# Uneven dV stores around one DMA engine, x in two pieces, and a reordered tail in a decode gradient kernel

## The chip, the cores and the metric

The kernel runs on one core of a Trainium2 chip. The metric is the device time of one execution in microseconds. A core has five compute engines (PE, the tensor engine; DVE, the vector engine; ACT, the scalar engine; POOL, the general engine; SP, which here only issues transfers) and sixteen DMA engines that carry all transfers. SP, ACT and POOL issue transfers, each into a queue of its own.

## The reference

The forward function mixes two branches over one token x of 640 numbers: a decode attention with 32 heads over a cache of 4096 keys and values of 128 numbers, and a dense layer with a Mish activation. The kernel computes the output and the gradients (a vector-Jacobian product with grad_out) of nine inputs.

```python
def forward(x, k_cache, v_cache, wq, wo, B_x, w1, b1, w2, gate_w):   # bfloat16
    g = sigmoid((x * gate_w).sum(-1, keepdims=True))
    q = (x @ wq).reshape(32 heads, 128)
    p = softmax(q . k_cache * 128 ** -0.5)           # 32 x 4096
    a = (p . v_cache).reshape(1, 4096) @ wo
    h = B_x @ w1 + b1
    b = (h * tanh(softplus(h))) @ w2
    return g * a + (1 - g) * b
# outputs: the result, then d/dx, dK, dV (each 32 x 4096 x 128), dwq, dwo, dw1, db1, dw2, dgate_w
```

K and V are read once (32 MB each) and dK and dV written once (32 MB each). With the weights and their gradients the page counts 82.03 MB read and 82.03 MB written.

## The kernel before

Heads are taken in 16 pairs; `NP` is 16 and `J` is 64. K or V of a pair is one tile of 128 partitions by 8192 bfloat16 numbers, 16 KB a row and 2 MB in all. There are seven such buffers (`bufs`, named `kv0` to `kv6`). A gradient is written over the tile that it belongs to: dV over V, dK over K, in four quarters by `outer` (line 465, on DVE), and then stored to memory from the same buffer. Free buffers wait in `free_q`. `pump` starts the next loads of a fixed list, all on SP, whenever a buffer is given back; the instruction on SP then waits until the store out of that buffer has landed. `store_kv` (line 736) issues one store and gives its buffer back; the stores go by POOL while loads are left and by SP afterwards.

The order of all other work is written out by hand. The function `slot(i, s)` has the sixteen steps of pair i: transposes of V and of the next K on PE (line 374) with copies out of PSUM on ACT (line 377), products for the scores and for dP (line 384), the softmax, column sums for o and dq (line 433), and the quarters of dV and dK. A table `side`, filled by `plan` and `at`, hangs the weights' work on these steps: the dense branch in pairs 0 to 6, and wo, wq and their gradients spread over the rest, in four groups of eight heads.

At the start POOL issues five small loads one after the other (line 185): x, gate_w, grad_out and b1 in two parts. At the end the last pair is written out without `slot`. The helper `last_dv(t)` makes quarter t of dV and, after the second and the fourth quarter, stores half of it through SP (line 875); `last_dk(t)` does the same for dK (line 881). Between them stand the rows of dwo (`dwo_row`, on ACT, stored through ACT by `st_dwo`), the last sums for dx (`dx_sum`, line 486), the last part of dwq (`dwq_row` on ACT, stored by `st_dwq` through POOL) and `o_rows` and `a_cols`, which turn the last heads' o into wo's products. Then a short chain of small steps makes the three small outputs out, dx and dgate_w: `fin` is collected on DVE (lines 918 to 935) with a sum over partitions on PE in between (`dg_ps`, line 928), transposed on PE (`fr_ps`, line 939), copied by DVE into `frow` (line 941) and stored by three transfers on POOL (line 944).

Of the kernel before, what the change touches and what calls it, by code (L numbers as in the profile page):

```python
# [17 lines left out]
def kernel(  # L18
# [34 lines left out]
    P = 128  # L53
    _, H, Sk, Dh = A_k_cache.shape
# [5 lines left out]
    J = 64  # L60
# [22 lines left out]
    dwo_v = out_5.rearrange("(g p k) n -> g p k n", p=P, k=8)  # L83
# [3 lines left out]
    def vec_cols(v):  # L87
        return v.rearrange("(p c) -> p c", c=RC)

    x_v = A_x.rearrange("a b (p c) -> (a b p) c", c=RC)  # L90
    dy_v = grad_out.rearrange("a b (p c) -> (a b p) c", c=RC)
# [10 lines left out]
    def C(shape, dt, name):  # L102
        return const.tile(shape, dt, name=name, tag=name)
# [3 lines left out]
    bufs = [big.tile([P, bufw.get(i, KVW)], BF16, name=f"kv{i}", tag=f"kv{i}") for i in range(NBUF)]  # L107
    wqa = big.tile([P, RC, H * Dh], BF16, name="wq", tag="wq")
    wob = [big.tile([P, 8, D], BF16, name=f"wo{i}", tag=f"wo{i}") for i in range(2)]
    tch = [chp.tile([P, 4, P, 2], BF16, name=f"tch{i}", tag=f"tch{i}") for i in range(NT)]  # L110

    xc = C([P, RC], BF16, "xc")
    dyc = C([P, RC], BF16, "dyc")
    gwc = C([P, RC], BF16, "gwc")
# [7 lines left out]
    kbuf, vbuf, mbuf = {}, {}, {}  # L122
# [48 lines left out]
    def pump():  # L171
        while loads and (free_q or not loads[0][0]):
            loads.popleft()[1]()
# [5 lines left out]
        base=0, pattern=[[-1, P]], channel_multiplier=1,  # L179
    )  # L180
    pump()
    for t, src in ((xc[:], x_v), (gwc[:], vec_cols(gate_w)), (dyc[:], dy_v),
                   (b1c[:, 0:FK], B_b1[0:FM].rearrange("(p k) -> p k", k=FK)),
                   (b1c[0:FR, FK:FN], B_b1[FM:F].rearrange("(p o) -> p o", o=1))):
        nc.gpsimd.dma_start(t, src)
# [34 lines left out]
    def misc(shape, dt, name):  # L220
        return one_ps.tile(shape, dt, name=name, tag="misc")

    def chain(shape, dt, name):
        return one_ps.tile(shape, dt, name=name, tag="chain")
# [99 lines left out]
    def o_rows(g):  # L324
        ps = misc([P, 16, 8], F32, "o8_ps")
        nc.tensor.matmul(ps[:].rearrange("p a b -> p (a b)"), lhsT=od16[:].rearrange("p a b -> p (a b)"), rhs=idb[:],
                         start=True, stop=True)
        o8m = two.tile([P, 16, 8], F32, name="o8m", tag="o8m", bufs=1)
        nc.vector.tensor_tensor(o8m[:], ps[:], m16[:].unsqueeze(2).to_broadcast([P, 16, 8]), ALU.mult)
        nc.vector.reduce_sum(o8f[:], o8m[:].rearrange("p a b -> p b a"), axis=AX.X)  # L330
        nc.vector.tensor_copy(o8[:], o8f[:])

    def a_cols(g, c0=0, c1=RC):
        if c0 == 0:
            mst["a"] = misc([P, RC + W], F32, "a_ps")
        ps = mst["a"][:, 0:RC]
        wv = wob[g % 2][:].rearrange("p k (n c) -> p k c n", c=RC)
        for c in range(c0, c1):
            for k in range(8):
                nc.tensor.matmul(mst["a"][:, c:c + W], lhsT=wv[:, k, c, :], rhs=o8[:, k:k + 1].to_broadcast([P, W]),  # L340
                                 start=(k == 0), stop=(k == 7))
        if c1 == RC:
            if g == 0:
                nc.vector.tensor_copy(a_acc[:], ps)
            else:
                nc.vector.tensor_tensor(a_acc[:], a_acc[:], ps, ALU.add)

    def scaled(eng, dst, src, col):
        if eng is nc.vector:
            nc.vector.tensor_scalar(dst, src, col, None, ALU.mult)  # L350
        else:
            nc.scalar.mul(dst, src, col)  # L352
# [1 line left out]
    def dwo_row(g, k, eng=nc.scalar):  # L354
        scaled(eng, wob[g % 2][:, k, :], da_bc[:], o8f[:, k:k + 1])

    def st_dwo(g, eng, k0=0, k1=8):
        eng.dma_start(dwo_v[g][:, k0:k1], wob[g % 2][:, k0:k1])


    def kview(b):
# [18 lines left out]
    def products(ps, src, c, col):  # L380
        for t in range(4):
            B = 4 * c + t
            for e in range(2):
                nc.tensor.matmul(ps[:, 4 * B:4 * B + W].rearrange("p (a b) -> p a b", b=4),  # L384
                                 lhsT=src[:, t, :, e],
                                 rhs=col[:, e, :, :].rearrange("p a b -> p (a b)").unsqueeze(1).to_broadcast([P, W // 4, 4]),
                                 start=(e == 0), stop=(e == 1))
# [74 lines left out]
    def outer(b, col, row, q):  # L462
        n = J // 4
        j0 = q * n
        nc.vector.tensor_tensor(  # L465
            kview(b)[:, j0:j0 + n, :].rearrange("p j (a b) -> p j a b", b=2),
            col[:, j0:j0 + n, :].unsqueeze(2).to_broadcast([P, n, Dh // 2, 2]),
            row.rearrange("p (a b) -> p a b", b=2).unsqueeze(1).to_broadcast([P, n, Dh // 2, 2]),
            ALU.mult)
# [5 lines left out]
    def dq_row(i):  # L475
        dqb = two.tile([P, 2], BF16, name="dqb", tag="dqb")
        nc.vector.tensor_copy(dqb[:], st[i]["dq"][:, 0:2])  # L477
        ps = chain([P, 2, P], BF16, "dqr_ps")
        for hh in range(2):
            nc.tensor.transpose(ps[:, hh, :], dqb[:, hh:hh + 1].to_broadcast([P, P]), idb[:])  # L480
        c = 256 * (i % 4)
        nc.scalar.copy(dqrow[(i // 4) % 2][:, c:c + 256].rearrange("p (a b) -> p a b", a=2), ps[:])
# [6 lines left out]
    def dwq_row(g, c0, c1, rc, eng=nc.scalar):  # L489
        scaled(eng, wqa[:, rc, g * GC + c0:g * GC + c1], dqrow[g % 2][:, c0:c1], xf[:, rc:rc + 1])  # L490

    def st_dwq(c0, c1, eng):
        eng.dma_start(dwq_v[:, :, c0:c1], wqa[:, :, c0:c1])
# [178 lines left out]
    for k in range(8):  # L672
        at(4, (6, 7, 9, 10, 11, 11, 13, 14)[k], dwo_row, 0, k, nc.vector if k in (4, 5, 6, 7) else nc.scalar)
    plan(4, {5: rows(mlp_dxb, 0), 7: rows(mlp_dxb, 1), 14: rows(mlp_dxb, 2)})
    plan(5, {0: [(st_dwo, 0, nc.gpsimd)], 1: [(ld_wo, 2)], 5: rows(mlp_dxb, 3), 7: rows(mlp_dxb, 4), 14: dx(0, 0, 0, GC, 0)})
    plan(4, {10: [(ld_wq, HC, 2 * HC, nc.scalar)]})
    plan(6, {0: [(st_dw1,)]})

    for g in range(NG - 1):
        i = 4 * g + 4  # L680
# [16 lines left out]
    for g in (2, 3):  # L697
        i = 4 * g
# [8 lines left out]
    g, i = NG - 1, NP - 2  # L707
# [14 lines left out]
    def run_products(i, s):  # L722
# [5 lines left out]
        else:  # L728
# [2 lines left out]
                S_ps[n] = one_ps.tile([P, 2 * J + W], F32, name="S", tag="S")  # L731
            products(S_ps[n], src, s - 8, qR[(n // 4) % 2][:, n % 4])

    def store_kv(dct, i, dst, eng):
        b = dct[i]
        eng.dma_start(dst, bufs[b][:, 0:J * Dh])  # L736
        free_q.append(b)
        pump()

# [3 lines left out]
    def slot(i, s):  # L743
# [16 lines left out]
        if chain_on:  # L760
            if s == 0:
                dq_row(i - 1)
            if s in (0, 1, 3):
                dk_quarter(i - 1, (0, 1, 3).index(s) + 1)
            if s == 3:
                store_kv(kbuf, i - 1, dKv[i - 1], nc.gpsimd if loads else nc.sync)
            if s == 2:
                soft_max(i)
            if s == 4:
                soft_maxt(i)  # L770
            if s == 7:
                soft_z(i)
# [9 lines left out]
        if s in (9, 10, 12, 13):  # L782
            outer(vbuf[i], st[i]["p"], Dr[(i // 4) % 2][:, i % 4, :], (9, 10, 12, 13).index(s))
            if s == 13:
                store_kv(vbuf, i, dVv[i], nc.gpsimd if loads else nc.sync)
# [81 lines left out]
    i, g = NP - 1, NG - 1  # L867
# [3 lines left out]
    def last_dv(t):  # L871
        outer(vbuf[i], st[i]["p"], Dr[g % 2][:, q, :], t)
        if t % 2:
            h = slice((t - 1) * KVW // 4, (t + 1) * KVW // 4)
            nc.sync.dma_start(dVv[i][:, h], bufs[vbuf[i]][:, h])

    def last_dk(t):
        outer(fb, st[i]["ds"], Qr[g % 2][:, q, :], t)
        if t % 2:
            h = slice((t - 1) * KVW // 4, (t + 1) * KVW // 4)  # L880
            nc.sync.dma_start(dKv[i][:, h], bufs[fb][:, h])
# [12 lines left out]
    last_dv(0)  # L894
    for rc in range(RC):
        dwq_row(g, CA, CB, rc)
    o_rows(g)
    dq_row(i)
    last_dv(1)
    a_cols(g)  # L900
    for k in range(8):
        dwo_row(g, k)
        if k % 4 == 3:
            st_dwo(g, nc.scalar, k - 3, k + 1)
    last_dv(2)
    last_dv(3)
    last_dk(0)
    last_dk(1)
    for rc in range(RC):
        dx_sum(g, NG + g, CB, GC, rc)  # L910
        dwq_row(g, CB, GC, rc)
    st_dwq(g * GC + CA, (g + 1) * GC, nc.gpsimd)
    last_dk(2)
    last_dk(3)

    fin = C([P, 3, RC], BF16, "fin")
    ga = C([P, RC], F32, "ga")
# [8 lines left out]
                                   accum_out=dgp[:])  # L926
    dg_ps = chain([P, 1], F32, "dg_ps")
    nc.tensor.matmul(dg_ps[:], lhsT=ones_f[:], rhs=dgp[:], start=True, stop=True)
    dz = C([P, 1], F32, "dz")
    nc.vector.tensor_scalar(dz[:], dg_ps[:], g_all[:], omg[:], ALU.mult, ALU.mult)  # L930
    nc.vector.tensor_scalar(fin[:, 2, :], xf[:], dz[:], None, ALU.mult)
# [5 lines left out]
    fr_ps = misc([3, RC, P], BF16, "fr_ps")  # L937
    for c in range(RC):
        nc.tensor.transpose(fr_ps[:, c, :], fin[:, :, c], idb[:])
    frow = C([3, P, RC], BF16, "frow")  # L940
    nc.vector.tensor_copy(frow[:].rearrange("r p c -> r c p"), fr_ps[:])
    for r, v in enumerate((out_0.rearrange("a b n -> (a b) n"), out_1.rearrange("a b n -> (a b) n"),
# [31 lines left out]
```

## Time and profile before

| what | value |
|---|---|
| median of three runs | 406.26 us (405.51 to 407.17) |
| the profiled execution | 405.83 us |
| its span, first to last instruction | 404.0 us |
| busy: PE, weight loads, DVE, ACT, POOL | 297.2, 272.9, 285.6, 246.8, 25.2 us |
| DMA: moved, mean rate | 164.88 MB, 408 GB/s |
| DMA queue q1 (SP) | 8832 packets, 94.08 MB |
| DMA queue q0 (POOL) | 5472 packets, 63.42 MB |
| DMA queue q10 (ACT) | 1602 packets, 6.56 MB |
| DMA queue q8 (instructions) | 44 packets, 0.72 MB |

The busy times are shares of one span and overlap. A transfer between a tile of 128 rows and memory is spread over the sixteen DMA engines; each engine moves its share, 8 rows for such a tile, and then reports on its own, so that a transfer has sixteen landing times and counts as landed with the last of them. In the profile's stretches, a busy share of 1.00 stands for all sixteen DMA engines and 0.06 for one.

### The profile page before, as it was taken

Reading aid. Unit: us, or ns where it says so; the run is one execution under the profiler, and the core shown is the slowest. Engines: PE = TensorE matmul, PEld = TensorE weight load, DVE = VectorE, ACT = ScalarE, POOL = GpSimd, SP = SyncE. Lnnn points to the kernel's source line nnn. Section 1 sums busy time; section 2 is a strip of 40 time slices with the busy share of each in tenths; the row PEclk is TensorE's granted clock in tenths of the full one; section 3 lists DMA queues with packets and bytes.
Section 4 is the critical chain, followed back from the end, with each engine's and each line's share of the span. In section 5 each row is a group of like instructions: output and inputs, shape, how many; then the busy total and the mean of one; then the engine's idle time right before and its main releaser. Section 6 shows DMA issues by size and latency. Waiting matters only on the chain.

```text
span 404.0 us, 13041 instructions
## 1 busy us (share of the span) xinstructions
PE 297.2 (74%) x5654; PEld 272.9 (68%) x5657; DVE 285.6 (71%) x618; ACT 246.8 (61%) x507; POOL 25.2 (6%) x50
## 2 busy tenths in 40 slices
PE   4878996998885888673989869732989897987110
PEld 3558986877775777673889769732789786886100
DVE  2767695699975969583797839642695988597930
ACT  3555462586668678761766567731567996876800
POOL 3000100002000101000001000000000100000020
PEclk9999997998999899986999989985899998999555
DMA  8999999999999999999999999999999999999991
GB/s 275 426 399 434 420 423 417 430 418 420 423 422 427 391 421 429 427 431 430 428 423 428 426 427 426 425 426 432 431 406 400 414 428 419 422 430 422 420 386 44
DMA packets 15963, 164.88 MB, mean 408 GB/s; under 512 B 1713, under 2 KB 1905, under 8 KB 6178
## 3 DMA queue, kind: packets, MB, share of 16 engines
q1 hardware_dynamic: 8832, 94.08, 55.7%
q0 software_dynamic: 5472, 63.42, 37.3%
q10 hardware_dynamic: 1602, 6.56, 4.1%
q8 instruction: 44, 0.72, 0.7%
q14 instruction: 13, 0.11, 0.1%
HBM read 82.03 MB, written 82.03 MB: 406 GB/s over the span
## 4 chain that ended last, share of the span: by engine, by line
DMA 34%; issue 23%; PE 20%; DVE 12%; ACT 5%; POOL 2%; SPq 1%; POOLq 0%; ACTq 0%; DVEq 0%
DMA wq<-in_A_wq_dram 10%; DMA out_dram<-kv 8%; PE tr L374 8%; DVE kv L465 7%; DMA wq<-in_B_w_dram 6%; DMA wo<-in_A_wo_dram 5%; DMA kv<-in_A_k_cache_dram 5%; ACT tch L377 2%; PE dP L384 2%; PE o L433 2%; PE S L384 2%; PE dq L433 1%; PE q_ps L277 1%; PE a_ps L340 1%; DVE wq L486 1%
## 5 line engine op out<-in xcount | busy, mean ns | idle before, releaser
L374 PE MATMUL tr<-idf,kv 128*128 128x128 f32 x1024 | 172.1, 294 | 36.0 <-DMA kv<-in_A_v_cache_dram 20.0
L377 ACT COPY tch<-tr 128x512 f32<-128x512 f32 x256 | 144.2, 587 | 83.8 <-PE tr L374 78.6
L374 PEld LDWEIGHTS tr<-idf,kv 128*128 128x128 f32 x1024 | 118.6, 150 | 41.7 <-issue 36.9
L384 PEld LDWEIGHTS <-tch 128*128 128x128 bf16 x2048 | 89.5, 99 | 27.9 <-ACT tch L377 21.8
L465 DVE TENSOR_TENSOR kv<-p_dup,Dr 128x2048 bf16<-128x2048 bf16 x64 | 76.7, 1220 | 4.4 <-ACT p_dup L424 4.1
L465 DVE TENSOR_TENSOR kv<-ds_dup,Qr 128x2048 bf16<-128x2048 bf16 x64 | 76.8, 1220 | 0.4
L433 PEld LDWEIGHTS <-kv 128*128 128x128 bf16 x2048 | 59.1, 97 | 2.7 <-issue 1.6
L384 PE MATMUL dP<-dR,tch 128*128 128x48 bf16 x1024 | 47.3, 185 | 9.3 <-ACT tch L377 9.0
L384 PE MATMUL S<-qR,tch 128*128 128x48 bf16 x1024 | 48.1, 187 | 6.9 <-ACT tch L377 5.7
L290 DVE SCALAR_TENSOR_TENSOR junk<-wo,da_bc 128x640 bf16<-128x640 bf16 x32 | 26.3, 822 | 13.5 <-DMA wo<-in_A_wo_dram 12.7
L433 PE MATMUL o<-e_m,kv 128*128 128x48 bf16 x1024 | 32.4, 186 | 0.2 <-issue 0.2
L433 PE MATMUL dq<-ds_m,kv 128*128 128x48 bf16 x1024 | 30.6, 183 | 2.1 <-DVE ds_m L455 1.9
L736 POOL DMA_DIRECT2D out_dram<-kv x25 | 13.4, 537 | 296.0 <-DVE kv L465 278.6
L352 ACT ACTIVATE wq<-dqrow,xf 128x1024 bf16<-128x1024 bf16 (+2 forms) x30 | 25.1, 860 | 1.2 <-DVE wq L486 0.8
L486 DVE SCALAR_TENSOR_TENSOR wq<-wq,dqrow 128x1024 bf16<-128x1024 bf16 (+2 forms) x30 | 25.1, 863 | 0.2
L439 DVE TENSOR_TENSOR o<-o,rz 128x2 f32<-128x2 f32 x16 | 2.5, 158 | 26.5 <-PE o L433 26.5
L398 DVE TENSOR_REDUCE m<-S 64x1 f32<-64x64 f32 x32 | 7.0, 219 | 15.8 <-PE S L384 15.6
L424 ACT ACTIVATE p_dup<-e_m,rz 64x128 bf16<-64x128 bf16 x32 | 12.7, 397 | 7.8 <-DVE rz L418 7.4
L352 ACT ACTIVATE wo<-da_bc,o8f 128x640 bf16<-128x640 bf16 x20 | 15.9, 824 | 1.5 <-PE a_ps L340 0.9
L406 DVE TENSOR_REDUCE negM<-mt 64x1 f32<-64x64 f32 x32 | 7.1, 222 | 11.5 <-PE mt L403 10.8
L480 PE MATMUL dqr_ps<-idb,dqb 128*128 128x128 bf16 x32 | 4.9, 241 | 13.7 <-DVE dqb L477 13.7
L459 ACT COPY ds_dup<-ds_m 64x128 bf16<-64x128 bf16 x32 | 9.5, 297 | 8.1 <-DVE ds_m L455 7.6
(163 smaller groups left out, 253.2 us busy)
## 6 DMA issues: line engine op xcount, KB each, us to landing
out_dram<-kv POOLq DMA_DIRECT2D x25, 2048.0 KB, 19.8
kv<-in_A_v_cache_dram SPq DMA_DIRECT2D x16, 2048.0 KB, 19.8
kv<-in_A_k_cache_dram SPq DMA_DIRECT2D x15, 2048.0 KB, 20.6
out_dram<-kv SPq DMA_DIRECT2D x5, 2048.0 KB, 26.2
wo<-in_A_wo_dram SPq DMA_DIRECT2D x4, 1280.0 KB, 20.9
out_dram<-kv SPq DMA_DIRECT2D x4, 1024.0 KB, 20.5
out_dram<-wo POOLq DMA_DIRECT2D x3, 1280.0 KB, 26.8
wq<-in_A_wq_dram SPq DMA_DIRECT2D x2, 1280.0 KB, 9.5
```

The costliest lines, as they stand in the source:

```text
L290: nc.vector.scalar_tensor_tensor(junk[:], in0=wob[g % 2][:, k, :], scalar=1.0, in1=da_bc[:], op0=ALU.mult, op1=ALU.mult, accum_out=do8[g % ...
L352: nc.scalar.mul(dst, src, col)
L374: nc.tensor.transpose(tp[:, t, :], src[:, 4 * c + t, :], idf[:])
L377: nc.scalar.copy(dst[:].rearrange("p a b e -> p (a b e)").bitcast(F32), tp[:].rearrange("p a b -> p (a b)"))
L384: nc.tensor.matmul(ps[:, 4 * B:4 * B + W].rearrange("p (a b) -> p a b", b=4), lhsT=src[:, t, :, e], rhs=col[:, e, :, :].rearrange("p a b - ...
L406: nc.vector.tensor_reduce(negM[HS[hh]], mt[HS[hh], 64 * hh:64 * hh + 64], axis=AX.X, op=ALU.max, negate=True)
L424: nc.scalar.activation(p[HS[hh]], e_m[i % 2][HS[hh], :, hh].unsqueeze(2).to_broadcast([64, J, 2]), ACT.Copy, scale=st[i]["rz"][HS[hh], hh: ...
L433: nc.tensor.matmul(st[i][key][:].rearrange("p (a b) -> p a b", b=2), lhsT=src[:, j, :], rhs=rhs[:, j, :].unsqueeze(1).to_broadcast([P, W / ...
L459: nc.scalar.copy(ds[HS[hh]], ds_m[i % 2][HS[hh], :, hh].unsqueeze(2).to_broadcast([64, J, 2]))
L465: nc.vector.tensor_tensor(kview(b)[:, j0:j0 + n, :].rearrange("p j (a b) -> p j a b", b=2), col[:, j0:j0 + n, :].unsqueeze(2).to_broadcast ...
L486: nc.vector.scalar_tensor_tensor(w, in0=w, scalar=1.0, in1=dqrow[g % 2][:, c0:c1], op0=ALU.mult, op1=ALU.mult, accum_out=dq_acc[:, rc, par ...
L736: eng.dma_start(dst, bufs[b][:, 0:J * Dh])
```

## The change

Three things change. First, `store_kv` stores dV of pairs 5 and 10 in three transfers instead of one: rows 0 to 1, 2 to 121 and 122 to 127 for pair 5, and rows 0 to 10, 11 to 115 and 116 to 127 for pair 10. They are issued one after the other on POOL, and by the change's own words the sizes are such that DMA engine 4 is left out of the large piece. Second, the load of x at the start becomes two loads, of rows 0 to 59 and 60 to 127. Third, in the tail `last_dv(1)` stands ahead of `o_rows` and `dq_row`, `last_dv(2)` ahead of `a_cols`, `last_dk(1)` behind the last sums for dx, and `last_dk(2)` and `last_dk(3)` stand inside the chain that makes the small outputs, behind the matmul of `dg_ps` and behind the transposes of `fr_ps`. The parameter `rows` that `st_dwo` gains has its default everywhere, which is one transfer as before.

```diff
-    for t, src in ((xc[:], x_v), (gwc[:], vec_cols(gate_w)), (dyc[:], dy_v),
+    for t, src in ((xc[0:60], x_v[0:60]), (xc[60:P], x_v[60:P]), (gwc[:], vec_cols(gate_w)), (dyc[:], dy_v),
...
-    def st_dwo(g, eng, k0=0, k1=8):
-        eng.dma_start(dwo_v[g][:, k0:k1], wob[g % 2][:, k0:k1])
+    def st_dwo(g, eng, k0=0, k1=8, rows=(P,)):
+        p0 = 0
+        for n in rows:
+            eng.dma_start(dwo_v[g][p0:p0 + n, k0:k1], wob[g % 2][p0:p0 + n, k0:k1])
+            p0 += n
...
+    uneven = {5: (2, 120, 6), 10: (11, 105, 12)}
+
     def store_kv(dct, i, dst, eng):
         b = dct[i]
-        eng.dma_start(dst, bufs[b][:, 0:J * Dh])
+        p0 = 0
+        for n in uneven.get(i, (P,)) if dct is vbuf else (P,):
+            eng.dma_start(dst[p0:p0 + n], bufs[b][p0:p0 + n, 0:J * Dh])
+            p0 += n
         free_q.append(b)
         pump()
...
     last_dv(0)
     for rc in range(RC):
         dwq_row(g, CA, CB, rc)
+    last_dv(1)
     o_rows(g)
     dq_row(i)
-    last_dv(1)
+    last_dv(2)
     a_cols(g)
     for k in range(8):
         dwo_row(g, k)
         if k % 4 == 3:
             st_dwo(g, nc.scalar, k - 3, k + 1)
-    last_dv(2)
     last_dv(3)
     last_dk(0)
-    last_dk(1)
     for rc in range(RC):
         dx_sum(g, NG + g, CB, GC, rc)
         dwq_row(g, CB, GC, rc)
     st_dwq(g * GC + CA, (g + 1) * GC, nc.gpsimd)
-    last_dk(2)
-    last_dk(3)
+    last_dk(1)
...
     nc.tensor.matmul(dg_ps[:], lhsT=ones_f[:], rhs=dgp[:], start=True, stop=True)
+    last_dk(2)
     dz = C([P, 1], F32, "dz")
...
         nc.tensor.transpose(fr_ps[:, c, :], fin[:, :, c], idb[:])
+    last_dk(3)
     frow = C([3, P, RC], BF16, "frow")
```

## The prediction

> **What bounds the kernel now.** I read the slices of the page first, then stretches of the end, then the waits of SP's queue, and last the landing times that the trace keeps of every transfer. The slices:
>
> ```profile
> DMA  8999999999999999999999999999999999999991
> GB/s 275 426 399 434 420 423 417 430 418 420 423 422 427 391 421 429 427 431 430 428 423 428 426 427 426 425 426 432 431 406 400 414 428 419 422 430 422 420 386 44
> ```
>
> The DMA engines are busy in every slice but the first and the last, at 400 to 434 GB/s, while the compute engines have idle tenths everywhere. So the transfers set the time, and a change pays only if it shortens the DMA engine that finishes last. The end by stretches (length, busy time of PE, PEld, DVE, ACT, POOL, granted clock, mean busy share of the 16 DMA engines, GB/s):
>
> ```profile
> 390.50:392.50 2.00, 0.00 (x0) 0.00 (x0) 0.00 (x0) 0.00 (x0) 0.31 (x1) 0.50 0.92 377
> 392.50:394.00 1.50, 0.00 (x0) 0.00 (x0) 0.00 (x0) 0.00 (x0) 0.00 (x0) 0.50 0.57 236
> 394.00:396.50 2.50, 0.00 (x0) 0.00 (x0) 0.00 (x0) 0.00 (x0) 0.00 (x0) 0.50 0.25 101
> 396.50:402.20 5.70, 0.00 (x0) 0.00 (x0) 0.00 (x0) 0.00 (x0) 0.00 (x0) 0.50 0.06 26
> 402.20:404.00 1.80, 0.00 (x0) 0.00 (x0) 0.00 (x0) 0.00 (x0) 0.00 (x0) 0.50 0.00 0
> ```
>
> No compute is left there. From 396.5 to 402.2 us the share is 0.06, one engine of sixteen, at 26 GB/s. The sixteen shares of the last transfer (second half of the last dK) land in three clusters: seven at 390.7 to 392.1, eight at 394.3 to 396.5, and one alone at 402.6. The span ends at 404.0, so 1.4 us follow the last landing.
>
> The lone engine is late all along. On an engine a packet starts 3 or 4 ns before the one ahead of it ends; linking packets so gives 16 chains, which I followed to 300 us. A 16 KB packet of the software queue (q0, POOL's stores) takes 611 to 622 ns on average on fifteen chains and 648 ns on one. The 44 instruction packets of q8 go in turn over eight of the other chains, about 1.34 us each with the delay of the packet behind: 5.5 x 1.34 = 7.4 us, which is why eight land later than seven. SP's waits, and the issues on POOL and SP around pair 10's dV, show what the late engine costs on the way:
>
> ```profile
> SPq L131 <- DMA out_dram<-kv: 287.6, 26, 21.4
> ```
> ```profile
> 265.47 0.53 POOL L736 DMA_DIRECT2D out_dram<-kv  x1 [11.52 <-DVE kv L465]
> ```
> ```profile
> 292.73 0.33 SPq L131 DMA_DIRECT2D kv<-in_A_v_cache_dram  x1
> 302.97 0.33 SPq L131 DMA_DIRECT2D kv<-in_A_k_cache_dram  x1
> ```
>
> The loads wait for stores to free buffers. The store issued at 265.47 has fifteen shares landed at 285.6, the last at 292.6; SP issues the load into that buffer at 292.73. At 300 to 304 us five of the fast chains then sit idle for 0.6 to 1.8 us each (DMA share 0.90).
>
> **The change part by part.** *Uneven dV stores.* By its own words the change leaves engine 4 out of the large pieces. A 128-row store gives each engine 8 rows. With one row per engine in a small piece, 8 rows on 15 engines for 120 and 7 rows for 105, engine 4 gets 1 + 0 + 1 rows of pair 5 and 1 + 0 + 1 of pair 10 if the pieces follow one another around the engines: 4 rows in place of 16, so 12 less, and twelve of the others get 1 more. If engine 4 is the slow chain, it saves 12 x 0.648 = 7.8 us; its packets end at 402.2, so at 394.4. The others pay 0.62 us: the latest of the middle cluster goes from 396.5 to 397.1 and is now last. The landing moves from 402.6 to 397.1, **minus 5.5 us**. More can't come of it: the middle cluster had no idle stretch as far as I followed it, and after 304 us the share of all sixteen is 1.01 (over 1 where packets overlap) until the clusters end.
>
> [...]
>
> That engine 4 is the slow one the trace doesn't say: it gives packets no engine. It excludes the eight chains that fetch instructions; the single-row store of dh_bc went over a chain of the other eight, the slow one's group.
>
> *More issues on POOL.* Four more store issues and one more x load, at 0.53 us each (the row above). The pieces behind the first are issued 0.5 and 1.1 us late, into a queue where a store takes 14.7 to 27.1 us to land (between 255 and 305 us), so nothing of it reaches the end; without that cover 2 x 1.1 us. Behind them on POOL stands w1's gradient for pair 5 (issued at 158.0, landing 187.8: the same cover) and for pair 10 the next store, 20 us off. The lanes of semaphores shift by one and then by two per split; each POOL transfer waits for the one eight before it, which had landed long ago in every case here. SP's loads into the two buffers (k8 and v13) now wait for three transfers each; they are in one queue, so the last piece decides. The gate weight, dy and bias load 0.5 us later on POOL; their consumers feed the first dV store at 41.3 us, and loads issued by 27.8 us keep the queue full to 72 us. Nothing; 0.5 us if that cover were gone.
>
> *Tail.* DVE's groups in the end (by form; busy us, mean ns, idle before):
>
> ```profile
> L465 DVE TENSOR_TENSOR kv<-ds_dup,Qr 128x2048 bf16<-128x2048 bf16 x5 | 5.9, 1222 | 0.0
> L465 DVE TENSOR_TENSOR kv<-p_dup,Dr 128x2048 bf16<-128x2048 bf16 x4 | 4.8, 1218 | 0.0
> L941 DVE COPY frow<-fr_ps 3x640 bf16<-3x640 bf16 x1 | 1.9, 1911 | 0.8 <-PE fr_ps L939 0.8
> ```
>
> At 1.13 us from start to start: dV's first store goes out 1.5 us earlier (372.7 for 374.2), o8f and with it ACT's eight wo rows come 0.5 us later, dV's second half 0.6 us earlier, and the last two dK quarters move behind the sums (1.73 us) and into the waits for dg_ps and fr_ps (0.74 and 0.79 us). dK's halves are issued 1.1 us later (384.8 for 383.7), the three small outputs 2.4 us earlier (386.9 for 389.3). On POOL st_dwq comes 0.5 us later, still ahead of the small outputs. The final 1 MB takes 8 x 0.309 = 2.5 us per engine; even the first engine to finish (390.7) reaches it at 388.2 only, 3.4 us after the later issue. So the reordering is worth nothing at the end; were the queue empty, it would cost 1.1 us.
>
> **Sum.** Span 404.0 - 5.5 = 398.5; the profiled execution's own time lies 1.83 us over its span (405.83), so 400.3; that execution is 0.43 us under the median of the three runs, so 400.8 against 406.26.
>
> **Rivals.** *The engine left out isn't the slow one.* The slow engine then keeps its 16 rows or gets one more: last landing 402.6 to 403.2, 406.3 to 406.9 against the median, no change that the measurement can tell. [...] A stronger form: large pieces cut into equal runs from engine 0 on, so that 2, 120, 6, 11, 105 and 12 rows all begin there. The last engine is then spared, and engine 4 carries 0 + 8 + 1 + 1 + 7 + 1 = 18 rows, 2 x 0.648 = 1.3 us more: 407.6. [...] Against: the slow chain shares a group with the single-row store's.
>
> *Slower: the pieces read SBUF across the engines' normal rows.* If the shift by 2 or 11 rows makes two engines read through the same opening, the large pieces slow by a factor f; an engine with 15 of their packets pays 15 x 0.611 x (f - 1) = 9.2 (f - 1) us. It eats the gain at f = 1.6 and at f = 2 leaves 406.3 as the last landing, 410.0 in all. Against: the 64-row store of w2, two engines on the same rows' neighbourhood, has 5 KB packets of 196 ns like the 128-row one. [...]
>
> *A piece falls on few engines.* 105 rows on one engine would be 105 x 0.62 = 65 us and hold the load of v13 for most of it; against this, the 64-row and 128-row transfers here all land in sixteen shares.
>
> **How the numbers follow.** Forecast 0.66, wrong engine 0.20, rows that collide 0.09, few engines 0.05. The first alone spans 399 to 403 (uncounted idle and fetches either way). About 0.5% (2 us) is what a measurement of this kernel can tell from no change. Faster: 0.66. Same: the wrong engine's 0.20, its worst form (1.3 us) included. Slower: 0.09 + 0.05 = 0.14. The range 399.0 to 407.6 takes both first cases; about 0.14 lies above it.
>
> **Right or wrong.** Right: the stretch with a share of 0.06 shrinks from 5.7 us to under 1, the load of v13 follows its buffer's fifteenth landed share closely, the POOL rows show three stores of 0.5 us. Wrong: one share still lands 6 us behind, or 16 KB packets of the pieces take far over 0.62 us.

## The result, and the profile after

The changed kernel is slower: 410.74 us (median of four runs, 409.89 to 411.80) against 406.01 us for the kernel before (four runs, 405.51 to 407.17). The ratio is 1.0109, with a 95% interval of 1.0087 to 1.0132. The profiled execution took 410.65 us, its span is 408.9 us; before it was 404.0. One execution of all that follow, the fourth with neighbouring rows in SBUF (417.08 us), fell in a slower state of the chip and is not in its ratio.

The slices of the page after (DMA share and rate):

```profile
DMA  7999999999999999999999999999999999999980
GB/s 258 425 396 431 421 424 406 425 426 420 425 423 420 409 421 429 421 401 421 433 422 430 425 423 424 423 419 385 406 384 425 426 422 425 417 429 421 415 349 28
```

A slice is 10.2 us. Three slices from 276 to 307 us have fallen to 385, 406 and 384 GB/s, and the one from 174 to 184 us to 401. These are the places where the pieces of pair 10 and of pair 5 are written. (The kernel before has 406 and 400 GB/s between 293 and 313 us, so the last of the three is in part its own.) The share stays at 9 there: the DMA engines aren't idle, their packets are slower. From 276 to 307 us a 16 KB packet of POOL's stores takes 692 ns on average, 639 in the kernel before, and one of SP's 645 in place of 614. The end by stretches (length, busy time of PE, PEld, DVE, ACT, POOL, granted clock, DMA share, GB/s):

```profile
394.50:397.00 2.50, 0.00 (x0) 0.00 (x0) 0.00 (x0) 0.00 (x0) 0.00 (x0) 0.50 0.82 315
397.00:400.60 3.60, 0.00 (x0) 0.00 (x0) 0.00 (x0) 0.00 (x0) 0.00 (x0) 0.50 0.26 107
400.60:407.20 6.60, 0.00 (x0) 0.00 (x0) 0.00 (x0) 0.00 (x0) 0.00 (x0) 0.50 0.06 26
407.20:408.90 1.70, 0.00 (x0) 0.00 (x0) 0.00 (x0) 0.00 (x0) 0.00 (x0) 0.50 0.00 0
```

The stretch with a share of 0.06, one engine alone at 26 GB/s, was to shrink from 5.7 us to under 1. It has grown to 6.6 us. The last share of the last transfer lands at 407.5 (402.6 before), the fifteenth at 400.6 (396.5). So the slow engine wasn't spared, and all the others are some 4 us late as well. The three stores of pair 10 on POOL, and the load that waits for them on SP:

```profile
269.28 1.59 POOL L743 DMA_DIRECT2D out_dram<-kv  x3 [15.48 <-DVE kv L468]
```
```profile
299.66 0.33 SPq L131 DMA_DIRECT2D kv<-in_A_v_cache_dram  x1
```

The issues cost what was foretold, 1.59 us for three. But the fifteenth share of the last piece lands at 291.6 and the last at 299.5, and the load goes out at 299.66, 7 us later than before.

Counting bytes gives the course of the loss: for each time I took from the packets how much later the changed kernel had moved as many bytes as the kernel before. It is 0.5 us behind at 165 us, before any piece, 1.5 at 200, 1.7 at 270, 3.6 at 300, 4.3 at 310, and 3.3 from 320 to 380. So pair 5's pieces cost 1.0 us of all engines' time, pair 10's up to 2.6 us, of which 1.6 us remain, and next to nothing is lost in between: 2.8 us in all. The figure is rough: an execution with no piece at all (the tail only, below) is 1.3 us behind at 340 us by the same count.

### The profile page after: what moved, and what is told of

It reads as the page before. It is cut to its first block, busy times and chain, and to the rows that moved or that the text cites. A ratio compares the mean times of both kernels' runs of the same rounds, so it can differ in the third digit from the quotient of the medians.

```text
span 408.9 us, 13054 instructions
## 1 busy us (share of the span) xinstructions
PE 294.6 (72%) x5654; PEld 271.9 (66%) x5657; DVE 285.3 (70%) x618; ACT 247.3 (60%) x507; POOL 27.7 (7%) x55
## 4 chain that ended last, share of the span: by engine, by line
DMA 47%; PE 20%; DVE 12%; issue 11%; ACT 4%; POOL 1%; SPq 1%; DVEq 0%; ACTq 0%; POOLq 0%
DMA kv<-in_A_k_cache_dram 17%; DMA out_dram<-kv 10%; DMA wq<-in_A_wq_dram 10%; PE tr L377 8%; DVE kv L468 7%; DMA wq<-in_B_w_dram 6%; DMA kv<-in_A_v_cache_dram 4%; PE o L436 3%; PE dP L387 2%; DVE junk L290 2%; PE S L387 2%; ACT tch L380 1%; PE a_ps L340 1%; PE q_ps L277 1%; PE dq L436 1%
## 5 line engine op out<-in xcount | busy, mean ns | idle before, releaser
L743 POOL DMA_DIRECT2D out_dram<-kv x29 | 15.5, 536 | 294.8 <-DVE kv L468 276.8
## 6 DMA issues: line engine op xcount, KB each, us to landing
wq<-in_A_wq_dram SPq DMA_DIRECT2D x2, 1280.0 KB, 10.2
```

The source lines that it names most:

```text
L743: eng.dma_start(dst[p0:p0 + n], bufs[b][p0:p0 + n, 0:J * Dh])
```

## The experiments

The ratios are against the kernel before, run on the same chip. All edits are to the kernel before unless said otherwise.

### Which part of the change costs

**Tail only.** The changed kernel with whole x and whole stores.

```diff
-    uneven = {5: (2, 120, 6), 10: (11, 105, 12)}
+    uneven = {}
-    for t, src in ((xc[0:60], x_v[0:60]), (xc[60:P], x_v[60:P]), (gwc[:], ...
+    for t, src in ((xc[:], x_v), (gwc[:], ...
```

> The changed kernel with whole x and whole dV stores: only the order of the tail is changed. Theory (the cost lies in the pieces): the tail ends under queued transfers, so 406 us within 0.5%, with the last landing at 402 to 403 as before and one engine alone for 5 to 6 us ahead of it. Rival (the tail's later dK halves cost the 4.7 us): 409 to 411, with the first share of the last transfer landing later than 390.7.

Measured: 406.24 us, ratio 0.9992 (0.9975 to 1.0010). The tail is worth nothing.

**Pieces only, whole x.**

```diff
+    uneven = {5: (2, 120, 6), 10: (11, 105, 12)}
...
-        eng.dma_start(dst, bufs[b][:, 0:J * Dh])
+        p0 = 0
+        for n in uneven.get(i, (P,)) if dct is vbuf else (P,):
+            eng.dma_start(dst[p0:p0 + n], bufs[b][p0:p0 + n, 0:J * Dh])
+            p0 += n
```

> The kernel before with nothing but the six dV pieces; x is one load of 128 rows. Theory (every piece is cut into equal runs from engine 0 on, so the engine spared doesn't depend on what went before; its large pieces read SBUF across the engines' usual rows and are slow): the same 410 to 411.5 as the changed kernel, one chain early after pair 5, one engine alone at the end for 5 to 7 us, 16 KB packets of the pieces at 650 to 800 ns. Rival (a cursor that earlier transfers move): another engine is left out than in the changed kernel; if that is the slow one, 400 to 404 and no lone engine at the end, and otherwise another group of chains is early.

Measured: 410.48 us, ratio 1.0109 (1.0082 to 1.0136), the same as the whole change. The split of x neither helps nor hurts: no position set by it, from which later pieces are dealt, decides which engine is left out. But the time is lost in part in another place than in the changed kernel. In the profiled execution engines stand idle for a load:

```profile
306.00:308.00 2.00, 1.54 (x29) 1.39 (x25) 1.97 (x4) 0.92 (x5) 0.00 (x0) 1.00 0.40 172
```
```profile
308.22 0.33 SPq L131 DMA_DIRECT2D kv<-in_A_k_cache_dram  x1
```

SP issues the load 0.1 us after the last share of a store has landed (308.1; the fifteenth at 306.4). By the count of bytes this execution is 3.3 us behind at 306 us and 5.4 at 310, while at the end its last engine is only 2.0 us behind the next, and not 6.9. So what the slow engine costs can be paid on the way, by engines that wait for it, or at the end.

### Which engine is left out, and which one is slow

How POOL's queue deals rows out can be counted. Its packets in the changed kernel and before, from the page (packets, MB, share of 16 engines):

```profile
q0 software_dynamic: 5616, 63.42, 37.4%
```
```profile
q0 software_dynamic: 5472, 63.42, 37.3%
```

With the pieces and whole x there are 112 packets more than before, all of 4 bytes. Four further transfers report landing on sixteen engines each, 64. The other 48 are just the empty places if each piece of n rows is dealt ceil(n / 16) to an engine and filled up: 14 for 2 rows (16 - 2), 8 for 120 (128 - 120), 10 for 6, 5 for 11, 7 for 105 (112 - 105) and 4 for 12. The split of x adds the other 32: sixteen landings and sixteen packets for the rows. The sizes show the dealing too. Of the 60 rows fifteen engines have 40 bytes (four rows of 10) and one has 16, four fillers in one packet; of the 68 rows thirteen have 50 bytes, one 38 (three rows and two fillers) and two 20, fillers alone. So rows go in runs of five to an engine, and the last engines are short. Were a piece dealt to fewer engines, with equal shares, it would need no fillers. So the last engine is the one left out, in every piece, and the first ones have a row of each small piece. The chain that first reaches the next store (at 169.4 us, the next at 173.9) has no row of any of the three pieces of pair 5.

**Marks.** To see where engines stand in this order, small loads of n rows into an unused tile were added, of a size that tells n.

```diff
+    def tags(i, eng, ns):
+        for n in ns:
+            c, w = sum(range(4, 4 + n)), 4 + n
+            eng.dma_start(tag[0:n, c:c + w], Kv[i][0:n, 0:w])
+    plan(3, {6: [(tags, 3, nc.sync, (1, 2, 4, 8))]})
+    plan(5, {5: [(tags, 5, nc.gpsimd, range(1, 16))]})
+    plan(8, {11: [(tags, 8, nc.gpsimd, range(1, 16))]})
```

> The kernel before with marks: POOL also loads n rows of 8 + 2n bytes for n = 1 to 15 into an unused tile, once in pair 5 and once in pair 8, and SP loads 1, 2, 4 and 8 such rows in pair 3. Nothing else is changed, and the marks cost little (406 to 409; 15 issues of 0.53 us on POOL). Linked to the chains of packets they show which engines n rows go to and which of them is the slow one. Theory: the n rows lie on engines 0 to n - 1, nested sets, one row each, so the first chain holds all fifteen sizes and the last none. [...]

Measured: 411.32 us, ratio 1.0131 (1.0091 to 1.0170), more than expected. POOL waited:

```profile
L711 POOL DMA_DIRECT2D tag<-in_A_k_cache_dram x30 | 15.0, 503 | 51.2 <-DMA out_dram<-kv 32.0 <-DMA out_dram<-wo 15.6 <-DMA tag<-in_A_k_cache_dram 3.5
```

The issues took 15.0 us as expected, the waits in front of them 51.2 us, and pair 5's store went out at 178.2 instead of 157.5. What the marks show doesn't hang on the time: each mark of n rows from 2 to 15 has n packets (one row each), and those that follow one another at once do so on the same chains, so the sets are nested and always begin at the same engine. The slow chain carries the mark of 8 rows of SP's queue, not those of 1, 2 and 4.

**Finer marks on SP's queue.** As above, with these plans only.

```diff
+    plan(3, {6: [(tags, 3, nc.sync, range(1, 16))]})
+    plan(5, {5: [(tags, 5, nc.gpsimd, (4, 8, 12))]})
```

> The kernel before with marks: in pair 3 SP loads n rows of 8 + 2n bytes for n = 1 to 15 into an unused tile, in pair 5 POOL loads 4, 8 and 12 such rows. A look at which chain carries which marks, not a time. The earlier marks put the slow chain among engines 4 to 7 of SP's queue. Theory (the change names the right engine): it carries the marks of 5 rows and more, so engine 4. Rival: it first appears with the marks of 6, 7 or 8 rows, so engine 5, 6 or 7, and the engine that the change spares is neither.

Seen: the marks of n = 1 to 8 on SP nest without a fault. One chain has 16 KB packets of 640 ns on average (the others 611 to 622, nearly each exactly 611); it carries the marks of 5 to 8 rows and none of 1 to 4. So the slow engine is the fifth in the order of these marks, number 4 counted from 0, as the change says. On POOL's queue it is among those with the mark of 8 rows and not among those with 4, which agrees. **The change aims at the right engine and spares another**, the sixteenth. Of pair 5's and 10's pieces the slow one writes 0 + 8 + 1 and 1 + 7 + 1 = 18 rows, where it had 16.

### Why the packets slow down

Two rows more on the slow engine are 2 x 0.648 = 1.3 us. Of the 4.7 us between the medians that leaves 3.4, of which the bytes show some 2.8 as a lag of all engines. I first took a collision of shifted rows for it.

**Shifted, no engine left out.**

```diff
+    uneven = {5: (2, 126), 10: (2, 126)}
```

> The kernel before with dV of pairs 5 and 10 stored as 2 and 126 rows. No engine is left out (8 rows on each of fifteen engines and 6 on one), but the 126 rows are shifted by two against the engines' usual rows. Theory (collision): packets of 16 KB at 650 to 800 ns after 157 and 266 us, and 408 to 410 in all, though the balance is as before. Rival (the uneven share is what costs): 405.5 to 407.

Measured: 408.79 us, ratio 1.0058 (1.0037 to 1.0080). The shares are as even as before to two rows, and half of the loss is there.

**Fifteen engines, the rows not shifted.**

```diff
+    uneven = {5: (120, 8), 10: (120, 8)}
```

> The kernel before with dV of pairs 5 and 10 stored as 120 and 8 rows. One engine is spared as in the change, but the 120 rows start at row 0, so fifteen engines read their usual rows. Theory (collision of shifted rows is most of the cost): 16 KB packets keep 611 to 622 ns around these stores, engines 0 to 7 carry two rows more, 406 to 408 in all. Rival (the uneven share or the number of pieces costs, not the shift): 409 to 411 as in the changed kernel.

Measured: 409.75 us, ratio 1.0110 (1.0070 to 1.0151). The theory as stated falls: with the 120 rows beginning at row 0 the loss is as large as in the change. (The slow engine writes 18 rows here too, so by its rows 1.3 us of the loss are its own.)

**The 120 rows alone.** The other 8 rows are not written.

```diff
+    uneven = {5: (120,), 10: (120,)}
```

> As the 120 and 8 rows, but the 8 rows of dV of pairs 5 and 10 are left out (they are not written). No piece is left whose rows lie close together; fifteen engines have their usual rows, one has none. Theory (the small pieces cost: 8 engines read from 8 neighbouring partitions at once): DMA keeps 420 to 430 GB/s in 165 to 180 and 270 to 290 us, and 405.5 to 407 in all. Rival (an engine that is out of step with the others costs): the rate falls in both stretches as in the 120 and 8 rows, to some 370 at 175 to 180, and 408 to 409.5 in all.

Measured: 408.48 us, ratio 1.0063 (1.0044 to 1.0082). So small pieces aren't needed either: here the slow engine has its 16 rows as before, fewer bytes are moved, and 0.6% is lost. Single 16 KB packets of POOL's stores take up to 2651 ns around pair 5's and 2822 ns around pair 10's; in the kernel before, no such packet took over 1015 ns from 155 to 185 and from 265 to 300 us.

**Two halves of 64 rows, and two halves by columns.**

```diff
+    uneven = {5: (64, 64), 10: (64, 64)}
```

> The kernel before with dV of pairs 5 and 10 stored as 64 and 64 rows: two transfers, every engine four rows of each, no engine left out and none out of step. [...] Rival (the number of transfers is all that matters, or out of step): 16 KB packets at 611 to 622, 405.5 to 407.

```diff
+        w = J * Dh // n            # n = 2 for dV of pairs 5 and 10
+        for t in range(n):
+            eng.dma_start(dst[:, t * w:(t + 1) * w], bufs[b][:, t * w:(t + 1) * w])
```

> The kernel before with dV of pairs 5 and 10 stored as two column halves of 128 rows each: two transfers, the same rows on every engine, all in step, packets of 8 KB. Theory (rows that lie close, or engines out of step): no loss, 405.5 to 407. Rival (each further transfer costs, whatever its rows): 407.5 to 409.5.

Measured: 408.98 us, ratio 1.0077 (1.0049 to 1.0104) for the halves of 64 rows, 406.53 us, 1.0006 (0.9989 to 1.0022) for the halves by columns. In both every engine has equal shares of two transfers. Here is pair 5's stretch (columns as above), before, of the 64 rows and of the columns:

```profile
175.00:180.00 5.00, 4.32 (x112) 4.17 (x111) 4.94 (x8) 3.49 (x8) 0.53 (x1) 1.00 1.01 429
```
```profile
170.00:175.00 5.00, 5.00 (x86) 4.90 (x85) 2.48 (x6) 3.31 (x5) 0.00 (x0) 0.75 1.04 394
175.00:180.00 5.00, 4.03 (x110) 3.88 (x108) 4.93 (x8) 3.49 (x8) 0.53 (x1) 1.00 0.99 364
```
```profile
170.00:175.00 5.00, 5.00 (x90) 4.91 (x88) 2.80 (x7) 3.47 (x5) 0.00 (x0) 0.73 1.02 433
175.00:180.00 5.00, 3.71 (x103) 3.57 (x100) 4.94 (x8) 3.62 (x7) 0.53 (x1) 1.00 1.02 431
```

At a full DMA share the 64 rows run at 364 GB/s, the column halves at 431. So it is neither the number of transfers nor an engine out of step. What is left is which rows an engine gets, or that the columns' packets are of 8 KB; the even and odd rows below, with 16 KB packets, take the second away.

**On which side?** Three more stores in two transfers of 64 rows: even and odd rows on both sides; neighbouring rows in SBUF to even and odd rows in memory; and the other way around.

```diff
+            for t in range(2):     # even_odd
+                eng.dma_start(dst.rearrange("(r two) n -> two r n", two=2)[t], bufs[b][t:P:2, 0:J * Dh])
+            for t in range(2):     # sbuf_64
+                eng.dma_start(dst.rearrange("(r two) n -> two r n", two=2)[t], bufs[b][64 * t:64 * t + 64, 0:J * Dh])
+            for t in range(2):     # memory_64
+                eng.dma_start(dst[64 * t:64 * t + 64], bufs[b][t:P:2, 0:J * Dh])
```

> The kernel before with dV of pairs 5 and 10 stored as its even rows and its odd rows, 64 each: two transfers, every engine four rows of each out of its usual eight, in SBUF and in memory. Theory (packets slow down where an engine's rows are not its usual ones): 420 to 430 GB/s between 165 and 180 us and 405.5 to 407. Rival (any two-piece store by rows costs): 370 to 400 GB/s there and 408 to 410, as the halves of 64 rows.

> As the halves of 64 neighbouring rows in SBUF, but written to the even and then the odd rows in memory (so these two tensors' rows come out permuted): on the memory side every engine keeps its usual region, on the SBUF side it does not. [...] Rival (memory side): no loss, 405.5 to 407.

> The other way around: even and odd rows in SBUF, written to rows 0 to 63 and 64 to 127 in memory (rows of these two tensors permuted). Theory (SBUF side): no loss, 420 to 430 GB/s, 405.5 to 407. Rival (memory side): 360 to 400 GB/s between 170 and 180 us, 408 to 410.

Measured: even and odd 406.88 us, ratio 1.0012 (0.9999 to 1.0026), at 413, 429 and 427 GB/s in the three parts from 165 to 180 us; neighbours in SBUF 1.0112 (1.0063 to 1.0161), from three runs of 409.5, 412.6 and 413.9; neighbours in memory 406.35 us, 0.9991 (0.9974 to 1.0009). The same stretch with neighbours in SBUF, then with neighbours in memory:

```profile
175.00:180.00 5.00, 3.74 (x104) 3.60 (x100) 4.94 (x8) 3.60 (x7) 0.53 (x1) 1.00 0.98 343
```
```profile
175.00:180.00 5.00, 4.74 (x122) 4.58 (x120) 4.94 (x6) 3.20 (x7) 0.53 (x1) 1.00 1.01 429
```

The loss arises on the SBUF side: 343 GB/s with neighbours there, 429 with neighbours in memory. Packets of 2.65 us with the 120 rows are 4.3 times 611 ns. If engines that hold each other up take turns evenly, that would be four of them and more, not two. This is an estimate from the two durations; no run shows the opening that the prediction supposes.

**Single packets.** Of dV of pairs 5 and 10 only two pieces of eight rows were stored.

```diff
+            for r, w in ((slice(96, 104), 8000), (slice(0, 32, 4), 7936))[::1 if i == 5 else -1]:
+                eng.dma_start(dst[r, 0:w], bufs[b][r, 0:w])
```

> The kernel before, but of dV of pairs 5 and 10 only two pieces of eight rows are stored, the rest is not written: rows 96 to 103 (packets of 16,000 B) and rows 0, 4, ... 28 (packets of 15,872 B), in this order in pair 5 and the other way around in pair 10. Eight engines write one row each in every piece. A look at the packets' durations; the time is no measure. [...] Rival (engines out of step with the others are slowed, whatever the rows): the same durations in both pieces.

Seen: in pair 5 the eight packets of neighbouring rows start between 164.9 and 168.2 us and take 1200, 2580, 2229, 596, 2778, 596, 1839 and 1742 ns. The eight of rows four apart, started from 166.6 to 171.1, take 592 each. In pair 10 the engines come to the neighbouring rows one after another, from 269.2 to 282.7 us, and the packets take 596 seven times and 638 once. So neighbouring rows are slow where several engines read them at the same time (five of pair 5's packets start within 0.8 us), and not by themselves. (In pair 10 two of the packets of rows four apart took 1072 and 1392 ns; I have no reason for these.)

**Quarters.**

```diff
+            for t in range(4):
+                r = slice(t, P, 4)                    # quarters_step4
+                r = slice(32 * t, 32 * t + 32)        # quarters_32
+                eng.dma_start(dst[r], bufs[b][r, 0:J * Dh])
```

> The kernel before with dV of pairs 5 and 10 stored in four pieces of 32 rows, rows t, t + 4, t + 8 and so on. [...] Rival (pieces of unusual rows cost by their number): 409 or more.

> The same in four pieces of 32 neighbouring rows. [...] Rival (number of pieces): the same time as by steps of four.

Measured: by steps of four 406.85 us, ratio 0.9997 (0.9981 to 1.0014); neighbours 409.71 us, 1.0068 (1.0044 to 1.0091). Pair 10's stretch before, by steps of four and with neighbours:

```profile
270.00:280.00 10.00, 1.40 (x12) 1.23 (x12) 0.00 (x0) 0.59 (x1) 0.00 (x0) 0.50 1.01 431
```
```profile
270.00:280.00 10.00, 1.41 (x12) 1.24 (x12) 0.34 (x1) 1.07 (x2) 0.40 (x1) 0.65 1.00 421
```
```profile
270.00:280.00 10.00, 1.41 (x12) 1.24 (x12) 0.00 (x0) 0.58 (x1) 0.00 (x0) 0.54 1.02 406
```

Four transfers in place of one don't matter (0.9997); which rows each takes does (1.0068). At 175 to 180 us the neighbours still ran at 424 GB/s; their loss shows only in pair 10 and after.

Taken together, the stores that take neighbouring rows in SBUF (2 and 126, 120 and 8, 120 alone, 64 and 64, four times 32) lost time, with ratios from 1.0058 to 1.0112, and those by columns or by every second or fourth row in SBUF lost nothing that could be measured, 0.9991 to 1.0012. That engines hold each other up when they read neighbouring rows at the same time is my estimate from the packets of eight neighbouring rows, up to 2778 ns in pair 5 and 596 to 638 in pair 10. Which partitions an engine read, and what it shares with others there, no trace here shows.

### Can the slow engine be relieved?

By the marks of 1 to 8 rows SP's queue too begins at the lowest engines, with one row on each. The theory here is that it deals 68 rows, a count that 16 doesn't divide, to four engines only, none of them the slow one.

```diff
-            nc.sync.dma_start(dKv[i][:, h], bufs[fb][:, h])
+            for a, b in ((0, 60), (60, P)):
+                nc.sync.dma_start(dKv[i][a:b, h], bufs[fb][a:b, h])
```

> The kernel before with the last two stores of SP's queue (dK's halves) each as 60 and 68 rows, and nothing else changed. Theory (SP's queue takes the largest divisor up to 16 on the lowest engines, and the slow engine is the fifth): 60 rows go four each to fifteen engines, 68 rows seventeen each to engines 0 to 3, so the slow engine writes 4 rows of 8 KB in place of 8, twice: 8 x 0.325 = 2.6 us less, last landing 400.0; engines 0 to 3 write 13 more rows twice, 26 x 0.309 = 8.0 us on top of some 391, 399 in all. 403 to 404.5. Rival (68 rows are spread five each over fourteen engines, as POOL's): the slow engine writes 9 rows for 8, 406.5 to 408.

Measured: 406.65 us, ratio 0.9998 (0.9978 to 1.0019). The end:

```profile
396.00:400.00 4.00, 0.00 (x0) 0.00 (x0) 0.00 (x0) 0.00 (x0) 0.00 (x0) 0.50 0.32 130
400.00:402.00 2.00, 0.00 (x0) 0.00 (x0) 0.00 (x0) 0.00 (x0) 0.00 (x0) 0.50 0.26 111
402.00:404.00 2.00, 0.00 (x0) 0.00 (x0) 0.00 (x0) 0.00 (x0) 0.00 (x0) 0.50 0.06 25
```

A share of 0.32 is five engines: the four with the 68 rows, which end between 401.6 and 403.3, and the slow one, which ends at 401.6. The dealing of the 68 rows is as expected, but the second 68 rows were issued only at 391.8, since SP waited for an earlier store, and the four engines became the last. Half as much was tried at two places:

```diff
+            for a, b in ((0, 60), (60, P)) if t == 1 else ((0, P),):        # in last_dk
+            for a, b in ((0, 60), (60, P)) if t == 3 else ((0, P),):        # in last_dv
```

> The kernel before with only the first half of the last dK stored as 60 and 68 rows. Both halves so ended even: the slow engine 0.7 us earlier, but engines 0 to 3, with 26 packets more, only at 402 to 403.6. Theory: with one half the slow engine saves 4 x 0.325 = 1.3 us and ends at 401.3, engines 0 to 3 carry 13 packets more (4.0 us) and end at 396 to 400; 404.5 to 405.6, faster by 0.2 to 0.4%. Rival (packets of four engines on 68 rows collide, or the queue of SP is held by the further transfer): 406 or more.

> The same with the second half of the last dV in place of dK's first half, one transfer earlier in SP's queue. Theory: the same 1.3 us less on the slow engine, and more time for engines 0 to 3; 404.5 to 405.6. Rival (collisions): 406 or more.

Measured: 405.59 us, ratio 0.9984 (0.9965 to 1.0003), and 405.69 us, 0.9992 (0.9969 to 1.0015). With dK's first half the last landing is at 401.6, close to the 401.3 worked out, and the median is 0.9 us lower; but the interval holds 1, so neither is shown to beat the kernel before.

## Why the prediction was wrong

**What bounds the kernel: right.** One late engine sets the end, and the order of the tail doesn't matter (0.9992 for the tail alone).

**The step that failed first: which engine is left out.** The term of 12 x 0.648 = 7.8 us, and with it the 5.5 us of gain, needs the slow engine to go from 16 rows to 4. It went to 18. The term rests on pieces that follow one another around the engines, which I assumed because the change's own words came true by it, and gave 0.66; no run shows such an order, nor the 4 rows. What the runs showed in its place is the rival's stronger form: every piece dealt from the first engine on in equal runs, 18 rows on the slow engine. Its price, 1.3 us, follows from the two rows and was not measured by itself (the 120 and 8 rows, 18 on the slow engine, and the 120 rows alone, 16, differ by 0.5%, but also by the bytes of the 8 rows). POOL's loads of 128 and 64 rows at the start of the kernel before can't tell the two apart: they have sixteen equal packets each (80 bytes, 8 rows of 10, and 8 bytes, 4 rows of 2). What I had right, that the change names the slow engine, was of no use. POOL's pieces and loads here go to all sixteen engines, each with a sixteenth of the rows, rounded up, with 48 fillers counted for the six pieces.

**The step that failed second: rows that collide, 0.09.** Slow packets in the pieces were named, and the price was of the right form: 9.2 (f - 1) us. But no run shows two engines on one opening, from which I took the slow packets to come; what the runs show in its place is the lag of 2.8 us by the bytes, which would be f = 1.3, and packets of up to 2.8 us with the 120 rows alone. The chance was too small, since I set against it the store of w2's 64 rows, whose packets were as fast as those of 128 rows (196 ns). That was no evidence on 16 KB packets with all engines in them at once: as pair 10's eight neighbouring rows show, such rows can give packets of 596 ns when the engines come to them one after another. I also thought of rows that are shifted, and the shift isn't needed: 120 and 8 rows from row 0 on lose as much (1.0110, and the pieces 1.0109).

**Treating these as rivals of each other was the third fault.** They add up: 406.0 + 1.3 + 2.8 = 410.1 us, where 410.7 was measured; the remaining 0.6 us is about the lag of 0.5 us that this execution had before any piece, and isn't explained further. The upper end of 407.6 took in only one of them. That the prediction's 410.0 for f = 2 lies close to the measured time is luck: it holds a gain of 5.5 us that didn't come and a loss of 9.2 us where the bytes show 2.8.

**POOL's issues and the waits: right in themselves.** Three stores take 1.55 and 1.59 us and delay nobody. The load behind pair 10 follows the last share and not the fifteenth, as the prediction had it for the case that it is wrong.

## What to carry to other kernels

Split a store from SBUF to memory by columns, or by every second or fourth row, and not into blocks of neighbouring rows: for two stores out of 32, and with the same number of transfers, the blocks cost 0.7 to 1.1% of the kernel's time here and the others nothing that could be measured (0.9991 to 1.0012). Before a row count is chosen to leave an engine out, count the 4-byte packets of such a transfer (here 48 fillers for six pieces): they show whether the rows go to all engines or to fewer; which engine is short, small loads of a size that tells n can show. And where two rivals of a forecast can happen together, their prices belong in one sum.

## What the runs showed of the hardware

In these runs POOL's queue filled a piece of n rows up to ceil(n / 16) places on each of sixteen engines with 4-byte packets (48 for the six pieces, all accounted for), while SP's queue put 68 rows on four engines (a DMA share of 0.32 from 396 to 400 us, with the slow engine as the fifth). Where eight engines read one each of eight neighbouring partitions within 5 us, a packet took up to 2778 ns; where they came one after another, 596 to 638. The slow engine is slow in nearly every packet of POOL's 16 KB stores, 624 to 665 ns for the middle half of them, where the median of each of the others is 611 ns; alone at the end of the kernel before, from 397.0 us, it took 309 ns for each 8 KB packet, the median of all.
